# Block 0 of a gated long-convolution and SwiGLU layer: first statistics on one engine, rows normed one by one, and the down products of the first row block in another chunk order

## The chip, the cores and the metric

The kernel runs on one core of a Trainium2 chip. A core has TensorE (PE, matrix products into PSUM), VectorE (DVE), ScalarE (ACT), GpSimd (POOL) and SyncE (SP), which here issues nearly all DMAs. The metric is the device time of one execution in microseconds; the median of several runs is compared. Trace times are microseconds from the start of the span.

## The reference

The input x is 2048 rows of D = 576. Six vectors of length D come from a condition c. The layer is a gated causal convolution followed by a SwiGLU network, each behind a layer norm that is scaled and shifted by those vectors:

```python
mod = (silu(c) @ w_mod)                  # sa, ca, ga, sb, cb, gb
h = layernorm(x) * (1 + ca) + sa
x = x + ga * A(h, k, v, shift_k, ssm_k, ssm_D)
h = layernorm(x) * (1 + cb) + sb
x = x + gb * ((silu(h @ w1) * (h @ w3)) @ w2)     # F = 4608
```

A multiplies h (the gate) with y: kv is k, shifted by four taps, times v; y is kv convolved over the 2048 rows with a filter of its own for each channel, plus kv times ssm_D. The reference does the convolution by FFT.

## The kernel before, in words

**Tiling.** The rows are eight blocks of 256. A block lies in SBUF as 128 partitions by 2 rows (`cc` 0 and 1) by 576. The convolution of a block is done in a transformed domain: `x_spectrum` (X, of kv) and `w_spectrum` (W, of the filter taps) are products with small bases on TensorE, copied out of PSUM by ScalarE (helper `forward`, lines 333 and 336). `v_block` combines W into V on VectorE; `pair` multiplies X and V of two blocks and adds into z; `inverse` (L572) brings z back. The SwiGLU part goes over four row blocks of 512 rows (`r` 0 to 3). `stream` computes h (F in 36 groups of 128, in 9 chunks of four) into `h3`; `down` multiplies h3 with w2 in two halves of 288 columns (`h`), nine chunks each, with w2 in a ring of four chunks.

**Block 0** is `first_block` (L661 to 746). Its instructions on VectorE, ScalarE and TensorE are tied to the order of the program by hand (`in_order`); what comes later is ordered by the framework's scheduler, with costs and due times that `advance` hands out. In program order it does this:

- The bases and taps are made; `warm` (L659) issues products that nobody reads, three, then four after the transposes of the taps (`k_rows`, L394).
- kv is built on VectorE, W of block 0 on TensorE (L333). The first layer norm needs mean and variance of two rows per partition. Row 1 has them from `quick_stats` on VectorE (L495 to L500: two partial statistics, one merge, EPS added, and a power on POOL). Row 0 has them later from `ln_sums` on ScalarE (L469, two passes with accumulators) and `ln_var` and `ln_shift` on POOL.
- X, V and z of block 0 follow, three of the six condition vectors (`mod_piece`, L238, and `arow` L249, `brow` L251), the normed rows `hg` on ScalarE (L723), `inverse`, and the gate on VectorE (L544, L546).
- `k_rows(1)` transposes the taps of block 1. `mod_columns` (L267) makes cb and sb as columns, by 60 matmuls of one column. Then come the four pieces of `w_spectrum(1)`.
- For each row the residual is added (`residual_row`, L579, L581), the second statistics are taken, and `normed` (L504) writes the row into `h2row`, which has 640 columns: the last 64 of the 576 twice. `turn_split` (L611) transposes five tiles of 128 on TensorE; the repeated columns make the fifth tile hold its 64 rows twice, at partitions 0 and 64. `turned_split` scales and shifts out of PSUM into `h2T`, tiles 0 to 2 on ScalarE (L623), 3 and 4 on VectorE (L620). Between them stand `warm` calls of six, two and three.

PSUM is four slots of one shape, given in turn to every product. `stream` for row block 0 then starts (L1014, L1025; h on ScalarE L1032 and L1036, VectorE L1039), with the rest of blocks 1, 2 and 3 on VectorE beside it. Its chunks become complete in the order 4, 5, 6, 0, 7, 1, 8, 2, 3, since six of them are first done for 256 rows alone. `down(0)` (L1134, w2 loaded by L1123) goes through the chunks in the order 0 to 8.

**Queues.** SP issues loads in order; a load waits there until its buffer is free. Transposing DMAs (L303, L819) and spills of X and V (L445, L449) stand in the same queue.

Of the kernel before, what the change touches and what calls it, by code (L numbers as in the profile page):

```python
# [21 lines left out]
H = 288  # L22
NF = F // P
# [4 lines left out]
W2C = 4  # L28
# [7 lines left out]
HEAD_PACE = 1.4  # L36
AHEAD = 2
EPS = 1e-5
TURN = 7
QUICK = False  # L40

# [7 lines left out]
class _Kernel:  # L49
# [205 lines left out]
    def mod_columns(self):  # L255

        nc = self.nc
        w5 = self.wm[:, 0:5 * 6 * D].rearrange("p (a d) -> p a d", a=5)
        ps = self.ps()
        for i, m in enumerate((4, 3)):  # L260
            for j in range(6):
                lo = min(P * j, 512)
                n = P if j < 4 else 64
                out = ps[0:n, i, j:j + 1] if j < 5 else ps[64:P, i, 4:5]
                for ct in range(5):
                    k = P if ct < 4 else 64
                    nc.tensor.matmul(out, w5[0:k, ct, m * D + lo:m * D + lo + n],  # L267
                                     self.crep[0:k, ct, 0:1], start=(ct == 0), stop=(ct == 4))
        nc.scalar.activation(self.cbcol[:], ps[:, 0, 0:5], ACT.Copy, bias=1.0)
        nc.scalar.copy(self.sbcol[:], ps[:, 1, 0:5])  # L270


    def load_kv(self, s, between=None):
# [315 lines left out]
    def normed(self, s, cc, m, r):  # L589

        row, x1 = self.h2row, self.xo[s]
        self.center(row[:, cc, 0:D], x1[:, cc, :], m, r)
        self.center(row[:, cc, D:640], x1[:, cc, 512:D], m, r)

    def normed_act(self, s, cc, r, b):
        row, x1 = self.h2row, self.xo[s]
        with self.behind(self.nc.scalar):
            for lo, hi, at in ((0, D, 0), (512, D, D)):
                self.nc.scalar.activation(row[:, cc, at:at + hi - lo], x1[:, cc, lo:hi], ACT.Identity,  # L599
                                          bias=b[:, cc:cc + 1], scale=r[:, cc:cc + 1])  # L600

    def turn(self, pt, cc):
        for ct in range(5):
            self.nc.tensor.transpose(pt[:, cc, ct * P:(ct + 1) * P],
                                     self.h2row[:, cc, ct * P:(ct + 1) * P], self.ident[:])

    def turn_split(self, cc):

        pt = [self.ps((P, 2, 1024), BF16) for _ in range(2)]
        for ct in range(5):  # L610
            self.nc.tensor.transpose(pt[ct // 3][:, 0, ct % 3 * P:(ct % 3 + 1) * P],  # L611
                                     self.h2row[:, cc, ct * P:(ct + 1) * P], self.ident[:])
        return pt

    def turned_split(self, pt, cc):
# [45 lines left out]
    def first_block(self):  # L661

        nc = self.nc
        since = len(nc.cur_bb.bb.instructions)
        x1 = self.xo[0]
        self.angles(nc.vector, 1)
        self.whole_turns(1)
        self.waves(1)
        self.shift_taps()
        self.whole_turns(0)  # L670

        ps = self.ps()
        nc.tensor.matmul(ps[0:64, 0, 0:5], self.drow[:], self.ident[0:9, 0:9:2], start=True, stop=True)
        nc.tensor.matmul(ps[64:P, 0, 0:4], self.drow[:], self.ident[0:9, 1:9:2], start=True, stop=True)
        nc.scalar.copy(self.dcol[:, 0:4], ps[:, 0, 0:4])
        nc.scalar.copy(self.dcol[0:64, 4:5], ps[0:64, 0, 4:5])
        tap = self.knat[:, :, 0]
        nc.gpsimd.tensor_add(tap, tap, self.dcol[:])
        self.waves(0)
        self.warm(3, self.h2T[0][:, 0, :])  # L680
        sums = [self.small.tile([P, 1], F32, name="l1" + k, tag="sr" + k) for k in "um"]
        self.run_all(self.k_rows(0))
        self.cond_silu()
        self.warm(4, self.h2T[0][:, 0, :])
        rows = self.kv_rows(0)
        for _ in range(4):
            next(rows)

        nc.vector.memset(self.wm[0:1, 3 * D:3 * D + 1], 0.0)
        self.load_mod(3, 2)  # L690
        self.load_k(1)
        self.run_all(self.w_spectrum(0))
        self.cond()
        self.run_all(rows)
        mean, rstd = self.quick_stats(x1[:, 1, :], "l1")
        nmr = self.small.tile([P, 1], F32, name="l1nm", tag="nmr1")
        nc.gpsimd.tensor_mul(nmr[:], mean, rstd)
        nc.gpsimd.tensor_single_scalar(nmr[:], nmr[:], -1.0, op=ALU.mult)
        self.run_all(self.x_spectrum(0))
        self.run_all(self.v_block(0))  # L700
        self.load_w13(0, 0)
        self.load_kv(1)
        self.load_x(1)
        self.load_w13(1, 1)
        self.load_gb()
        self.whole_turns(0, True)
        self.waves(0, True)
        X, V = self.X[0], self.V[0]
        self.accs[0] = z = self.acc.tile([P, 6, D], BF16, name="z0", tag="z0")
        for o in (0, 3):  # L710
            nc.vector.tensor_add(X[:, o, :], X[:, o + 1, :], X[:, o + 2, :])
            nc.vector.tensor_mul(z[:, o:o + 3, :], X[:, o:o + 3, :], V[:, o:o + 3, :])
            nc.vector.tensor_add(z[:, o + 1, :], z[:, o, :], z[:, o + 1, :])
            nc.vector.tensor_sub(z[:, o, :], z[:, o, :], z[:, o + 2, :])
        self.mod_piece(2)
        self.ln_sums(x1, 0, sums[0], sums[1], 0)
        scales = [self.ln_shift(*self.ln_var(*sums, "l1", nc.gpsimd), nc.gpsimd), (rstd, nmr)]
        for m in (1, 0):
            self.mod_piece(m)
        self.hg[0] = hg = self.lnp.tile([P, 2, D], BF16, name="hg", tag="hg", bufs=2)  # L720
        for cc in range(2):
            r, b = scales[cc]
            nc.scalar.activation(hg[:, cc, :], x1[:, cc, :], ACT.Identity, bias=b[:, 0:1], scale=r[:, 0:1])  # L723
        ps = [self.inverse(0, cc) for cc in range(2)]
        self.run_all(self.gate(0))
        self.run_all(self.k_rows(1))
        self.mod_columns()
        self.run_all(self.w_spectrum(1))
        self.residual_row(0, 0, ps[0])
        st = [self.quick_stats(x1[:, 0, :], "l2")]  # L730
        self.residual_row(0, 1, ps[1])
        st.append(self.quick_stats(x1[:, 1, :], "l2"))
        self.normed(0, 0, *st[0])
        busy = self.shk[:, 0, 0:512]
        self.warm(6, busy)
        pt = self.turn_split(0)
        self.warm(2, busy)
        self.normed(0, 1, *st[1])
        self.turned_split(pt, 0)
        pt = self.turn_split(1)  # L740
        self.warm(3, busy)
        self.turned_split(pt, 1)
        self.accs.pop(0)
        self.hg.pop(0)
        self.start = since
        return self.in_order(since, [e.engine for e in (nc.vector, nc.scalar, nc.tensor)])[nc.vector.engine]
# [367 lines left out]
    def down(self, r, rate):  # L1114
        nc = self.nc
        for h in range(2):
# [1 line left out]
            tail = r == NRB - 1 and h == 1  # L1118
            accs = [self.ps() for _ in range(4 if tail else 2)]
            acc = [accs[t][:, 0, 0:H] if tail else accs[t // 2][:, t % 2, 0:H] for t in range(4)]  # L1120
            for f0 in range(0, NF, W2C):
                w = _ap(self.w2m, (h * NF + f0) // W2C % NW2 * W2C * H, [[H, W2C], [1, H]])
                nc.sync.dma_start(w, self.w2[f0 * P:(f0 + W2C) * P, h * H:(h + 1) * H]  # L1123
                                  .rearrange("(a p) d -> p a d", p=P))
                last = f0 + W2C == NF
                if h == 0 and last:
                    self.last_w2 = self.newest()
                order = [(f, t) for f in range(W2C) for t in range(4)]
                if f0 == 0:
                    order = [(f, t) for t0 in (0, 2) for f in range(W2C) for t in (t0, t0 + 1)]  # L1130
                if last:
                    order = [(f, t) for t in range(4) for f in range(W2C)]
                for f, t in order:
                    nc.tensor.matmul(acc[t],  # L1134
                                     self.h3[:, f0 + f, t * P:(t + 1) * P], w[:, f, :],
                                     start=(f0 + f == 0), stop=(f0 + f == NF - 1))
# [12 lines left out]
                self.advance(rate * W2C * 4 * 0.126)  # L1149
# [127 lines left out]
```

## Time and profile before

| what | value |
|---|---|
| median of 5 runs | 510.14 us (509.44 to 510.79) |
| profiled execution | 510.79 us, its span 509.0 us |
| TensorE busy | 491.5 us, 97% of the span |
| VectorE busy | 339.3 us, 67% |
| ScalarE busy | 284.1 us, 56% |
| GpSimd busy | 23.2 us, 5% |
| mean granted clock of TensorE | 0.992 |
| DMA | 107.97 MB, mean 212 GB/s |

The profile is that of one execution. A timeline row gives start, duration, engine, line, operation, what it writes and reads, shapes and count, and in brackets how long the engine stood idle and what ended that. A chain is followed back from the last instruction to what released it. Ends of matmuls are modelled, so matmuls that follow each other overlap in the records: from start to start is the better spacing. The clock column is the share of TensorE's full clock that was granted; in the first 12.5 us it has no record of its own and shows 1.00, although 512-column products there start 0.43 us apart.

### The profile page before, as it was taken

The numbers are of one execution on the slowest core, as the hardware profiler recorded it, in microseconds if no ns is written. First come the engines' busy times: TensorE is split into PE (matmuls) and PEld (weight loads), VectorE is DVE, ScalarE is ACT, GpSimd is POOL, SyncE is SP. The second block draws the span as 40 slices with busy tenths as digits, with TensorE's granted clock in tenths as the row PEclk, the third lists the DMA queues.
The fourth block names the chain that finished last, engine by engine and source line by source line (L and its number), as shares of the span: only waits on it lengthen the run. The fifth ranks groups of instructions, "written<-read, shape, count | busy, mean of one in ns | idle before, by whom it ended". The sixth has DMA issues, their size and how long they took to land.

```text
span 509.0 us, 8873 instructions
## 1 busy us (share of the span) xinstructions
PE 491.5 (97%) x3530; PEld 288.2 (57%) x3530; DVE 339.3 (67%) x448; ACT 284.1 (56%) x565; POOL 23.2 (5%) x43
## 2 busy tenths in 40 slices
PE   6999989999998999999999999999999999999996
PEld 2767865547676444343777543434677544444774
DVE  8789899897998675999157999789771311112012
ACT  5839669758352579578560365975825255555000
POOL 4200000000001000000000000000000000000000
PEclk9979999999999999999999999999999999999999
DMA  8978887658999895448799996735475554460562
GB/s 272 332 199 211 255 315 221 197 176 264 258 366 294 286 315 181 158 109 270 205 272 332 313 319 226 217 104 175 140 188 124 172 176 137 145 187 0 140 171 62
DMA packets 115036, 107.97 MB, mean 212 GB/s; under 512 B 20339, under 2 KB 107572, under 8 KB 114996
## 3 DMA queue, kind: packets, MB, share of 16 engines
q1 hardware_dynamic: 114974, 107.41, 70.3%
q8 instruction: 27, 0.44, 0.4%
q14 instruction: 13, 0.11, 0.1%
q10 hardware_dynamic: 22, 0.01, 0.0%
HBM read 92.46 MB, written 9.44 MB: 200 GB/s over the span
## 4 chain that ended last, share of the span: by engine, by line
PE 63%; DVE 18%; DMA 7%; ACT 6%; issue 3%; SPq 2%; POOL 1%; POOLq 0%; DVEq 0%; ACTq 0%
PE ps L1014 25%; PE ps L1078 14%; PE ps L1134 14%; PE ps L1025 4%; DVE p L438 3%; DMA V<-Vd 2%; DVE z L440 2%; ACT junk L469 2%; DVE h L1039 2%; PE ps L333 2%; DVE z L433 2%; DVE og L1159 1%; PE ps L347 1%; DMA kh<-in_A_k_dram 1%; DMA wst<-in_B_w_dram 1%
## 5 line engine op out<-in xcount | busy, mean ns | idle before, releaser
L1014 PE MATMUL ps<-h2T,wst 128*128 128x512 bf16 (+1 forms) x1056 | 200.8, 341 | 0.9 <-ACT X L349 0.2
L1134 PE MATMUL ps<-wst,h 128*128 128x288 bf16 x1152 | 145.3, 286 | 4.7 <-DMA wst<-in_B_w_dram 3.2
L1014 PEld LDWEIGHTS <-wst 128*128 128x128 bf16 x1056 | 100.2, 98 | 86.8 <-issue 15.3
L1134 PEld LDWEIGHTS <-h 128*128 128x128 bf16 x1152 | 112.4, 98 | 36.2 <-issue 6.2
L1032 ACT ACTIVATE h<-ps 128x512 bf16<-128x512 f32 x108 | 64.8, 600 | 78.9 <-PE ps L1025 50.7
L1078 PE MATMUL ps<-h2T,wst 64*128 64x512 bf16 x648 | 70.3, 376 | 0.0
L1036 ACT CAST u<-ps 128x512 bf16<-128x512 f32 x108 | 63.4, 587 | 0.0
L438 DVE TENSOR_TENSOR p<-X,V 128x3456 bf16<-128x3456 bf16 x28 | 54.8, 1956 | 4.9 <-DMA V<-Vd 3.4
L440 DVE TENSOR_TENSOR z<-z,p 128x3456 bf16<-128x3456 bf16 x28 | 54.7, 1954 | 0.1
L1078 PEld LDWEIGHTS <-wst 64*128 64x128 bf16 x648 | 31.3, 94 | 38.3 <-DVE og L1159 0.2
L1105 DVE TENSOR_TENSOR h<-h,u 128x1024 bf16<-128x1024 bf16 x18 | 12.5, 692 | 58.1 <-ACT u L1102 58.1
L1039 DVE TENSOR_TENSOR h<-h,u 128x1024 bf16<-128x1024 bf16 x54 | 37.0, 687 | 12.9 <-ACT u L1036 12.9
L1099 ACT ACTIVATE h<-ps 128x512 bf16<-128x512 f32 x36 | 21.5, 597 | 39.8 <-PE ps L1078 39.8
L469 ACT ACTIVATE junk<-x 128x576 bf16<-128x576 bf16 x54 | 37.1, 687 | 3.1 <-DVE x L587 2.6
L1159 DVE TENSOR_TENSOR og<-ps,gbrow 128x576 bf16<-128x576 f32 (+1 forms) x18 | 12.3, 689 | 36.2 <-PE ps L1134 35.7
L1025 PE MATMUL ps<-h2T,wst 64*128 64x512 bf16 (+1 forms) x264 | 33.3, 341 | 0.1
L1102 ACT CAST u<-ps 128x512 bf16<-128x512 f32 x36 | 20.9, 581 | 0.0
L1025 PEld LDWEIGHTS <-wst 64*128 64x128 bf16 x264 | 8.5, 94 | 21.5 <-issue 18.1
L834 ACT ACTIVATE h2T<-h2T,sbcol,cbcol 128x256 bf16<-128x256 bf16 x20 | 10.4, 589 | 17.9 <-DMA h2T<-h2row 17.9
L599 ACT ACTIVATE h2row<-x,l2n,l2r 128x576 bf16<-128x576 bf16 (+1 forms) x24 | 13.7, 643 | 10.0 <-DVE l2n L487 10.0
L367 DVE TENSOR_TENSOR kv<-kv,p 128x1152 bf16<-128x1152 bf16 x24 | 18.1, 755 | 0.3
L361 DVE TENSOR_TENSOR p<-kh,shk 128x3456 bf16<-128x3456 bf16 x8 | 15.6, 1953 | 1.1 <-DMA kh<-in_A_k_dram 1.1
(142 smaller groups left out, 368.2 us busy)
## 6 DMA issues: line engine op xcount, KB each, us to landing
wst<-in_B_w_dram SPq DMA_DIRECT2D x80, 512.0 KB, 4.8
wst<-in_B_w_dram SPq DMA_DIRECT2D x72, 288.0 KB, 3.9
wst<-in_B_w_dram SPq DMA_DIRECT2D x80, 64.0 KB, 3.5
kh<-in_A_k_dram SPq DMA_DIRECT2D x7, 720.0 KB, 7.1
X<-Xd SPq DMA_DIRECT2D x5, 864.0 KB, 6.7
V<-Vd SPq DMA_DIRECT2D x5, 864.0 KB, 5.6
Xd<-X SPq DMA_DIRECT2D x4, 864.0 KB, 8.3
Vd<-V SPq DMA_DIRECT2D x4, 864.0 KB, 5.6
```

The lines of the kernel that those rows point to most:

```text
L438: nc.vector.tensor_mul(p[:], X[:], V[:])
L440: nc.vector.tensor_add(z[:], z[:], p[:])
L469: self.nc.scalar.activation(junk[:], src[:, i, :], func, scale=scale, accum_out=out[:, col:col + 1])
L1014: nc.tensor.matmul(gus[k][:, i, a * n:(a + 1) * n], w[:, 5 * i + ct, (fi + a) * P:(fi + a + 1) * P], hT[:, ct, t0:t1], start=(first and ct ...
L1025: nc.tensor.matmul(gus[k][:, i, a * n:(a + 1) * n], w[rows, 4, (fi + a) * P:(fi + a + 1) * P], hT[rows, 4, t0:t1], start=(first and a == 0 ...
L1032: nc.scalar.activation(self.h3[:, f:f + m, t0:t1], gus[k][:, 0, :].rearrange("p (a t) -> p a t", a=m), ACT.Silu)
L1036: nc.scalar.copy(self.u[:, k % 2, :], gus[k][:, 1, :])
L1039: nc.vector.tensor_mul(h3, h3, self.u[:].rearrange("p b (a t) -> p (b a) t", a=m))
L1078: nc.tensor.matmul(gus[k][:, i, :], ws[fc][rows, 5 * i + ct if ct < 4 else 4, cols], hT[rows, ct, :], start=swap == 0 and ct == 4, stop=sw ...
L1099: nc.scalar.activation(h3, gus[k][:, 0, :], ACT.Silu)
L1102: nc.scalar.copy(self.u[:, k % 2, :], gus.pop(k)[:, 1, :])
L1134: nc.tensor.matmul(acc[t], self.h3[:, f0 + f, t * P:(t + 1) * P], w[:, f, :], start=(f0 + f == 0), stop=(f0 + f == NF - 1))
```

## The change

1. Both rows of block 0 have their first statistics from `quick_stats` on VectorE; `ln_sums` on ScalarE and the five small POOL operations behind it go.
2. `mod_columns` multiplies with 64 equal columns instead of one, and reads every 64th.
3. `normed` no longer writes the repeated columns. `turn_tile` transposes the 64 last columns twice, into partitions 0 and 64. `normed_act`, for later blocks, still writes them.
4. In block 0 the order of the residual, the second statistics, the normed rows and `w_spectrum(1)` changes: row 0 is normed before row 1's statistics, two pieces of the spectrum stand ahead of the first turn and two behind it.
5. `warm` calls go from 3, 4, 6, 2, 3 products to 6, 3, 0, 0, 3.
6. `down(0)` goes through the chunks in the order of `FIRST`.

```diff
+FIRST = (4, 5, 6, 0, 7, 1, 8, 2, 3)
...
-                out = ps[0:n, i, j:j + 1] if j < 5 else ps[64:P, i, 4:5]
+                out = ps[0:n, i, 64 * j:64 * j + 64] if j < 5 else ps[64:P, i, 256:320]
...
-                                     self.crep[0:k, ct, 0:1], start=(ct == 0), stop=(ct == 4))
-        nc.scalar.activation(self.cbcol[:], ps[:, 0, 0:5], ACT.Copy, bias=1.0)
-        nc.scalar.copy(self.sbcol[:], ps[:, 1, 0:5])
+                                     self.crep[0:k, ct, 0:64], start=(ct == 0), stop=(ct == 4))
+        nc.scalar.activation(self.cbcol[:], ps[:, 0, 0:320:64], ACT.Copy, bias=1.0)
+        nc.scalar.copy(self.sbcol[:], ps[:, 1, 0:320:64])
...
-        self.center(row[:, cc, D:640], x1[:, cc, 512:D], m, r)
...
+    def turn_tile(self, dst, cc, ct):
+
+        n = P if ct < 4 else 64
+        for at in range(0, P, n):
+            self.nc.tensor.transpose(dst[at:at + n], self.h2row[:, cc, ct * P:ct * P + n], self.ident[:])
...
-        self.warm(3, self.h2T[0][:, 0, :])
-        sums = [self.small.tile([P, 1], F32, name="l1" + k, tag="sr" + k) for k in "um"]
+        self.warm(6, self.h2T[0][:, 0, :])
         self.run_all(self.k_rows(0))
         self.cond_silu()
-        self.warm(4, self.h2T[0][:, 0, :])
+        self.warm(3, self.h2T[0][:, 0, :])
...
-        mean, rstd = self.quick_stats(x1[:, 1, :], "l1")
-        nmr = self.small.tile([P, 1], F32, name="l1nm", tag="nmr1")
-        nc.gpsimd.tensor_mul(nmr[:], mean, rstd)
-        nc.gpsimd.tensor_single_scalar(nmr[:], nmr[:], -1.0, op=ALU.mult)
+        scales = []
+        for cc in range(2):
+            mean, rstd = self.quick_stats(x1[:, cc, :], "l1")
+            nmr = self.small.tile([P, 1], F32, name="l1nm", tag="nmr1")
+            nc.gpsimd.tensor_mul(nmr[:], mean, rstd)
+            nc.gpsimd.tensor_single_scalar(nmr[:], nmr[:], -1.0, op=ALU.mult)
+            scales.append((rstd, nmr))
...
-        self.ln_sums(x1, 0, sums[0], sums[1], 0)
-        scales = [self.ln_shift(*self.ln_var(*sums, "l1", nc.gpsimd), nc.gpsimd), (rstd, nmr)]
...
-        self.run_all(self.w_spectrum(1))
         self.residual_row(0, 0, ps[0])
-        st = [self.quick_stats(x1[:, 0, :], "l2")]
+        st = self.quick_stats(x1[:, 0, :], "l2")
         self.residual_row(0, 1, ps[1])
-        st.append(self.quick_stats(x1[:, 1, :], "l2"))
-        self.normed(0, 0, *st[0])
+        self.normed(0, 0, *st)
         busy = self.shk[:, 0, 0:512]
-        self.warm(6, busy)
+        spectrum = self.w_spectrum(1)
+        for _ in range(2):
+            next(spectrum)
         pt = self.turn_split(0)
-        self.warm(2, busy)
-        self.normed(0, 1, *st[1])
+        self.normed(0, 1, *self.quick_stats(x1[:, 1, :], "l2"))
         self.turned_split(pt, 0)
+        self.run_all(spectrum)
         pt = self.turn_split(1)
...
-            for f0 in range(0, NF, W2C):
+            for n, fc in enumerate(FIRST if r == 0 else range(NF // W2C)):
+                f0 = n * W2C
                 w = _ap(self.w2m, (h * NF + f0) // W2C % NW2 * W2C * H, [[H, W2C], [1, H]])
-                nc.sync.dma_start(w, self.w2[f0 * P:(f0 + W2C) * P, h * H:(h + 1) * H]
+                nc.sync.dma_start(w, self.w2[fc * W2C * P:(fc + 1) * W2C * P, h * H:(h + 1) * H]
...
-                                     self.h3[:, f0 + f, t * P:(t + 1) * P], w[:, f, :],
+                                     self.h3[:, fc * W2C + f, t * P:(t + 1) * P], w[:, f, :],
```

More of the change, by code (lines that the diff above doesn't have):

```diff
@@ L600, in normed_act @@
                                           bias=b[:, cc:cc + 1], scale=r[:, cc:cc + 1])
+    def turn_tile(self, dst, cc, ct):
+        n = P if ct < 4 else 64
+        for at in range(0, P, n):
+            self.nc.tensor.transpose(dst[at:at + n], self.h2row[:, cc, ct * P:ct * P + n], self.ident[:])
     def turn(self, pt, cc):
         for ct in range(5):
-            self.nc.tensor.transpose(pt[:, cc, ct * P:(ct + 1) * P],
-                                     self.h2row[:, cc, ct * P:(ct + 1) * P], self.ident[:])
+            self.turn_tile(pt[:, cc, ct * P:(ct + 1) * P], cc, ct)
     def turn_split(self, cc):
@@ L610, in turn_split @@
         for ct in range(5):
-            self.nc.tensor.transpose(pt[ct // 3][:, 0, ct % 3 * P:(ct % 3 + 1) * P],
-                                     self.h2row[:, cc, ct * P:(ct + 1) * P], self.ident[:])
+            self.turn_tile(pt[ct // 3][:, 0, ct % 3 * P:(ct % 3 + 1) * P], cc, ct)
         return pt
```

## The prediction, made before the changed kernel was built or run

> **What bounds the kernel now.** First I read the chain of work that ended last. It runs through TensorE for nearly the whole of block 0 (to 35 us), so there a saved microsecond of TensorE counts until another engine is later.
>
> ```profile
> 20.78 2.18 PE ps L572 x16
> 22.96 0.56 PE ps L394 x10
> 23.52 3.79 PE ps L267 x60
> 27.30 3.95 PE ps L333 x16
> 31.25 2.21 PE ps L659 x6
> 33.46 0.18 PE ps L611 x3
> ```
>
> Columns: start, us, what. Sixteen matmuls of L333 take 2.07 at 14.52 by the same chain, but 3.95 at 27.30. The windows view says why (columns: window; busy of PE, weight loads, DVE, ACT, POOL; granted clock; DMA share; GB/s):
>
> ```profile
> 19.32:22.73 3.41, 3.41 (x27) 2.29 (x27) 3.31 (x6) 1.18 (x5) 2.56 (x5) 1.00 1.14 330
> 22.73:26.14 3.41, 3.41 (x60) 3.09 (x59) 1.90 (x4) 2.47 (x3) 0.00 (x0) 1.00 1.00 384
> 26.14:29.56 3.42, 3.42 (x25) 2.49 (x26) 3.25 (x8) 1.05 (x4) 0.55 (x1) 0.50 1.11 319
> 29.56:32.97 3.41, 3.41 (x13) 1.66 (x11) 2.39 (x9) 1.73 (x3) 0.66 (x1) 0.50 1.22 222
> 32.97:36.38 3.41, 3.33 (x24) 1.72 (x23) 2.44 (x5) 2.20 (x6) 0.00 (x0) 1.00 0.28 78
> ```
>
> The clock is halved from 26.14 to 32.97, after the stretch filled by mod_columns' one-column matmuls. Third, the timeline of the same place, with what each waited for in brackets:
>
> ```profile
> 22.57 0.87 ACT L723 ACTIVATE hg<-x,l1n,l1r 128x576 bf16<-128x576 bf16 x1 [2.20 <-POOL l1n L487]
> 24.23 0.76 DVE L544 TENSOR_TENSOR hg<-hg,arow 128x1152 bf16<-128x1152 bf16 x1 [1.37 <-ACT hg L723]
> 30.78 0.63 DVE L504 TENSOR_SCALAR h2row<-x,l2mv,l2r 128x576 bf16<-128x576 bf16 x2
> 33.73 2.20 ACT L623 ACTIVATE h2T<-ps,sbcol,cbcol 128x128 bf16<-128x128 bf16 x6 [1.80 <-PE ps L611]
> 33.85 1.28 DVE L620 TENSOR_SCALAR h2T<-ps,cbcol,sbcol 128x128 bf16<-128x128 bf16 x4 [1.57 <-PE ps L611]
> ```
>
> VectorE stands 1.37 us for ScalarE's normed row, and later 1.57 us for the transposes, which stand behind the slow L333 and six L659 fillers. Last, the down stage of row block 0:
>
> ```profile
> 125.39 6.39 PE L1134 MATMUL ps<-wst,h 128*128 128x288 bf16 x50
> 132.91 7.77 PE L1134 MATMUL ps<-wst,h 128*128 128x288 bf16 x62 [1.13 <-DVE h L1039]
> ...
> 156.63 8.00 PE L1134 MATMUL ps<-wst,h 128*128 128x288 bf16 x64 [1.96 <-DMA wst<-in_B_w_dram]
> 164.84 0.38 PE L1014 MATMUL ps<-h2T,wst 128*128 128x512 bf16 x1 [0.21 <-ACT h2T L834]
> ```
>
> After 50 matmuls (three chunks and two) it waits 1.13 for the last gated chunk, which VectorE finishes late; then 1.96 for a weight chunk.
>
> **The parts.**
>
> *Head.* Six fillers from 5.41 instead of three: four 512-column fillers start 0.43 apart (1.71 for 4), so they end near 8.0, before the transposes at 8.58 that wait for POOL: nothing. Three instead of four after k_rows: L333 can start at 10.99, when kT's copy ends (9.87 + 1.12), not 11.33. Its reader is VectorE, which is later by the next part: counted nothing.
>
> *Both first statistics on VectorE.* One set takes 1.17 from start to next instruction (27.16 to 28.33). The second would push L415 from 14.30 to 12.21 + 2 x 1.17 = 14.55. The 0.84 idle before L415 hides most; L422 waited until about 14.81 for a W copy anyway, and now starts at 14.55 + 0.39 = 14.94, 0.08 late. So all of z is 0.08 late, and brow (22.10) goes to 22.18. On ScalarE two passes of 0.70 and two reads of about 0.2 go; on POOL five operations (0.94, 0.41, 0.43, 0.59, 0.19) go, and three (0.56, 0.19, 0.39), early and unhurried, come. hg now follows ga: 18.24 + 0.66 + two of 0.86 = about 20.6, before brow ends. L544 then starts at 22.18 + 0.67 = 22.86 instead of 24.23: **-1.37 on VectorE**. What is late next is brow, VectorE's own work.
>
> *Residual and second norm on VectorE.* The same spacing as before puts L579 for row 0 at 24.51, its statistics at 25.79, L579 for row 1 at 26.96. POOL's power ends 27.7; the first normed row starts at 28.24 (29.61 - 1.37) and costs 0.43 without the repeated columns (0.30 less, twice). The second set now stands behind it: 28.58 to 29.83; power to 30.58, a wait of about 0.75 before the second normed row at 30.61. Behind that wait stand the two turned pieces, then kv_rows(1). Normed ends 31.04; turned(0)'s two at 30.97 and 31.23.
>
> *TensorE.* mod_columns ends near 27.3, or 27.0 if its last part is not at half clock. A one-column matmul takes 63 ns (3.79 / 60) and a 128-column one 56 (0.56 / 10), so columns hardly set the price: 0, with -0.35 and +1.6 (27 ns more on each of 60) as ends. The Trainium skill, "TensorE: Matmul & The Clock Gate", section "Back-to-back issue gap", puts 1 to 64 columns at one price; by it the sum is 0 as well. Two pieces of L333 (8 matmuls, half of 2.07) fit from 27.3 to 28.3; the second needs PSUM that L579 frees at 27.7. Turn 0 waits for VectorE until 28.7. The other two pieces fill 29.1 to 30.1. Turn 1 waits for VectorE: 31.1, its last tiles 31.6 (bank freed by turned(0)). Twelve transposes for ten: two of 56 ns, hidden in that wait. Eight fillers (6 and 2) go; the last three are hidden by ScalarE.
>
> *ScalarE.* W copies end 29.1; turned(0) 29.1 to 30.3; W copies to 31.4; turned(1) 31.4 to 32.6 (three, 0.34 apart). The stream flows from there, where it did at 35.95: 3.3 earlier. VectorE starts kv_rows(1) at about 32.5, not 35.05: 2.5 earlier. Up to 66 us both count, x_spectrum joining them near 44; I take **-2.6**, ends -2.4 and -3.3. In stream 0's second half the normed rows of block 1 lose 0.29 twice, before a wait for kh at 64.85: nothing.
>
> *Down in chunk order.* The 1.13 wait goes, as the late chunks 2 and 3 come eighth and ninth, 14 us on (7 x 1.96). Late next is w2: its loads wait behind SP's transposing DMAs (issued 129.96 to 133.10), and the seventh chunk's load leaves at 133.20 for about 5.4 to landing, as before. After that the DMA wait of 1.96 at 156.63 can simply grow, with DMA share near 1. What comes through is bounded by 0 and -1.29 (with the semaphore's time); nearest is the turn at 164.84, whose chain had VectorE idle 0.77 for inverse L572: I take **-0.3**.
>
> Sum against the profiled execution (span 509.0, time 510.79): -2.6 - 0.3 = -2.9, 507.9. That execution lies 0.65 over the median 510.14, so the median of the runs becomes about 507.2.
>
> **The clock, and a rule against the change.** 288 columns stream in 0.1225 us, so 64 take 27 ns: about 0.4 of mod_columns' time, against 0.006 with one column. The window 152.44 to 155.86, with 18 matmuls of 288 columns (2.2 of 3.4 us), kept clock 1.00, so I take the clock to hold; 0.4 itself is not shown. At 23 us ten transposes run 56 ns apart at clock 1.00. The same page, "Part 4: PE-mode transpose", says that transposes don't count as TensorE activity the same way. By it the stretch after 29.5, where real fillers give way to transposes and waits, could let the clock fall: the sum would be the first rival's, not the forecast; no row separates the two.
>
> **Rivals.**
> 1. *The clock halves anyway.* For it: 0.4 is below what any window shows kept. Then the first two pieces end at 29.2, turn 0 at 29.8, the other two pieces at 31.8, the stream starts at 33.6, and may run at half to 36.4 (cost half of 2.8, 1.4). Gain 2.3 to 0.9, with the 0.3 or without: median 507.5 to 509.2, say 508.6.
> 2. *A transfer takes the place.* In the first 32 us the DMA share is about 1.0, and VectorE already waits 0.31 for kh at 64.85. If that load (issued 57.91, 6.92 to landing) does not move, the wait grows by all of the gain: about 510. Against: SP's waits from 36 to 66 us are 10.2 of L965 for TensorE, so loads move with TensorE.
> 3. *Slower: the order after block 0.* From 36 us the framework's schedule sets it, and it may come out otherwise. The place is VectorE between 143.9 and 157, on the chain to the turn at 164.84: two products of 1.95 already stand in it. Each further one ahead of L487 costs 1.95 there, one for one as TensorE waits for that turn. One leaves 0.95 of the gain; from two on it is slower: +1.0, median 511.1. Against: nothing in the change names these instructions.
>
> **Numbers.** Forecast 0.60 (505.6 to 507.7); rival 1: 0.17; rival 2: 0.13, which is also the case that block 0's end was covered; rival 3: 0.10. A measurement tells 0.2% (1.0 us) from nothing. Faster 0.60 + 0.17 = 0.77, within 0.13, slower 0.10. The low end is -3.3 - 1.29 from 510.14, 505.6; the high end reaches over rival 1 and most of rival 2, 510.0.
>
> **What would show it.** Clock 1.00 from 26 to 36 us; L544 at about 22.9 with no wait for ScalarE; first stream matmul near 32.6, L361 near 32.5; no wait for h L1039 in the first down stage, but longer ones for w2. Wrong if the clock row shows 0.50 there, if kh's wait at 64.85 grows, or if the turn's landing near 164 stays.

## The result, and the profile after

| | before | after |
|---|---|---|
| median of the runs | 509.91 us (507.16 to 512.72, 80 runs) | 508.21 us (505.85 to 511.14, 43 runs) |
| profiled execution, its span | 510.79 us, 509.0 us | 506.55 us, 504.7 us |
| mean granted clock of that execution | 0.992 | 0.999 |

The ratio of after to before is 0.9964 [0.9956, 0.9972]: the change makes the kernel 0.36% faster, about 1.8 us (the two medians lie 1.7 apart). The forecast for the median was 2.9 us less. The two profiled executions lie 4.24 us apart, more than twice the distance of the medians, because before's was taken 0.9 above its median and after's 1.7 below. So this pair of traces must not be read as the result, and below several profiles of each kernel stand side by side.

Line numbers move a little: L333, L394, L267, L572 and L659 of before are L334, L395, L268, L573 and L663 in after, L544 is L545, L504 is L505, L620 is L624, L361 is L362, L1039 is L1043, the transposes of block 0's rows (L611) are L606, and the matmuls of `stream` and `down` (L1014, L1134) are L1018 and L1139.

The chain of waits of after at the end of block 0 (start, us, what) answers to the one of before:

```profile
23.00 0.56 PE ps L395 x10
23.56 4.28 PE ps L268 x60
27.83 0.61 PE ps L334 x4
28.46 0.67 ACT W L337 x2
```

The chain no longer stays on TensorE. Sixteen matmuls of the spectrum at half clock and six fillers stood behind `mod_columns` before. Now the chain leaves TensorE for ScalarE at 28.4. But the 60 matmuls of `mod_columns` take 4.28 us in this view, where they took 3.79 with their last part at half clock. The windows of the same stretch (window; busy of PE, weight loads, DVE, ACT, POOL; granted clock; DMA share; GB/s):

```profile
22.66:26.07 3.41, 3.41 (x52) 2.74 (x50) 3.20 (x6) 1.12 (x1) 0.00 (x0) 1.00 1.01 378
26.07:29.49 3.42, 3.35 (x39) 2.39 (x37) 3.26 (x10) 1.25 (x4) 0.56 (x1) 1.00 1.11 324
29.49:32.90 3.41, 3.12 (x24) 1.60 (x23) 2.27 (x7) 3.33 (x9) 0.55 (x1) 1.00 1.31 218
```

The clock column reads 1.00 where before had 0.50 for two windows. In this execution it is 1.00 until 503.9, 0.8 us before the end. VectorE in the same place:

```profile
22.81 0.75 DVE L545 TENSOR_TENSOR hg<-hg,arow 128x1152 bf16<-128x1152 bf16 x1
28.07 0.42 DVE L505 TENSOR_SCALAR h2row<-x,l2mv,l2r 128x576 bf16<-128x576 bf16 x1
30.32 0.43 DVE L505 TENSOR_SCALAR h2row<-x,l2mv,l2r 128x576 bf16<-128x576 bf16 x1 [0.66 <-POOL l2r L501]
31.72 0.59 DVE L624 TENSOR_SCALAR h2T<-ps,cbcol,sbcol 128x128 bf16<-128x128 bf16 x2 [0.47 <-PE ps L606]
32.23 1.95 DVE L362 TENSOR_TENSOR p<-kh,shk 128x3456 bf16<-128x3456 bf16 x1
```

L545 starts at 22.81 and waits for nothing. The wait for the second POOL power (0.66) and the one for the last transposes (0.47) are new places, but short. L362 starts at 32.23, where it did at 35.05. Last, the down stage of row block 0 on TensorE:

```profile
122.05 13.88 PE L1139 MATMUL ps<-wst,h 128*128 128x288 bf16 x112
...
149.22 2.12 PE L1139 MATMUL ps<-wst,h 128*128 128x288 bf16 x16 [1.37 <-DMA wst<-in_B_w_dram]
152.33 8.00 PE L1139 MATMUL ps<-wst,h 128*128 128x288 bf16 x64 [0.99 <-DMA wst<-in_B_w_dram]
160.17 0.38 PE L1018 MATMUL ps<-h2T,wst 128*128 128x512 bf16 x1
160.80 2.12 PE L1139 MATMUL ps<-wst,h 128*128 128x288 bf16 x16 [0.25 <-DMA wst<-in_B_w_dram]
```

The first 112 matmuls, seven chunks, run through: the wait of 1.13 for h is gone. In its place the second half waits three times for w2, 2.61 together, where before had one wait of 1.96.

### The profile page after: what moved, and what is told of

Its sections match the earlier page's. It is cut to its first block, busy times and chain, and to the rows that moved or that the text cites. A ratio compares the mean times of both kernels' runs of the same rounds, so it can differ in the third digit from the quotient of the medians.

```text
span 504.7 us, 8868 instructions
## 1 busy us (share of the span) xinstructions
PE 487.8 (97%) x3528; PEld 286.0 (57%) x3528; DVE 339.1 (67%) x448; ACT 282.3 (56%) x561; POOL 22.3 (4%) x41
## 4 chain that ended last, share of the span: by engine, by line
PE 62%; DVE 20%; DMA 6%; ACT 5%; issue 3%; SPq 2%; POOL 1%; POOLq 0%; DVEq 0%; ACTq 0%
PE ps L1018 26%; PE ps L1139 15%; PE ps L1082 14%; PE ps L1029 4%; DVE p L439 3%; DMA V<-Vd 2%; DVE z L441 2%; DMA kh<-in_A_k_dram 2%; DMA wst<-in_B_w_dram 2%; ACT junk L470 2%; DVE z L434 2%; DVE og L1164 2%; DVE h L1043 1%; PE ps L348 1%; SPq L823 1%
## 5 line engine op out<-in xcount | busy, mean ns | idle before, releaser
L1018 PE MATMUL ps<-h2T,wst 128*128 128x512 bf16 (+1 forms) x1056 | 200.6, 341 | 0.4 <-ACT X L350 0.2
L1139 PE MATMUL ps<-wst,h 128*128 128x288 bf16 x1152 | 145.4, 286 | 4.0 <-DMA wst<-in_B_w_dram 3.5
L1018 PEld LDWEIGHTS <-wst 128*128 128x128 bf16 x1056 | 100.2, 98 | 86.3 <-issue 14.5
L1139 PEld LDWEIGHTS <-h 128*128 128x128 bf16 x1152 | 112.5, 98 | 35.2 <-issue 6.4
L1043 DVE TENSOR_TENSOR h<-h,u 128x1024 bf16<-128x1024 bf16 x54 | 37.0, 687 | 12.7 <-ACT u L1040 12.7
L470 ACT ACTIVATE junk<-x 128x576 bf16<-128x576 bf16 x52 | 35.7, 687 | 3.1 <-DVE x L588 2.6
L362 DVE TENSOR_TENSOR p<-kh,shk 128x3456 bf16<-128x3456 bf16 x8 | 15.6, 1954 | 1.0 <-DMA kh<-in_A_k_dram 1.0
## 6 DMA issues: line engine op xcount, KB each, us to landing
wst<-in_B_w_dram SPq DMA_DIRECT2D x80, 512.0 KB, 4.8
```

The source lines that it names most:

```text
L470: self.nc.scalar.activation(junk[:], src[:, i, :], func, scale=scale, accum_out=out[:, col:col + 1])
L1018: nc.tensor.matmul(gus[k][:, i, a * n:(a + 1) * n], w[:, 5 * i + ct, (fi + a) * P:(fi + a + 1) * P], hT[:, ct, t0:t1], start=(first and ct ...
L1043: nc.vector.tensor_mul(h3, h3, self.u[:].rearrange("p b (a t) -> p (b a) t", a=m))
L1139: nc.tensor.matmul(acc[t], self.h3[:, fc * W2C + f, t * P:(t + 1) * P], w[:, f, :], start=(f0 + f == 0), stop=(f0 + f == NF - 1))
```

## The experiments

**How they are read.** The first product of each `kv_rows` (L361 in before) stands at a fixed place in every kernel, so the time from one to the next splits the span into stretches. Below, "0 to 1" is the time from that product of block 0 to that of block 1, and so on. The stretch 2 to 3 (38.48 or 38.49) and the stretch 6 to 7 (33.74 to 33.76) are the same in all of them to 0.02 us, and are left out; "to the end" is from the product of block 0 to the end of the span. The clock column lists the windows of 3.41 us of half clock found in the trace; a piece of one in the last 2.5 us of the span, which most traces have, is left out. All in us, from one profiled execution each.

| kernel | 0 to 1 | 1 to 2 | 3 to 4 | 4 to 5 | 5 to 6 | 7 to end | to the end | half-clock windows |
|---|---|---|---|---|---|---|---|---|
| before | 28.56 | 29.80 | 55.02 | 52.03 | 99.23 | 165.64 | 502.51 | 2 in block 0 |
| before_again | 28.50 | 30.13 | 54.52 | 52.34 | 99.46 | 166.39 | 503.57 | 2 in block 0 |
| first_only | 28.31 | 30.20 | 54.15 | 52.53 | 100.03 | 165.75 | 503.21 | 2 in block 0 |
| stats_only | 27.35 | 29.47 | 54.45 | 52.17 | 99.06 | 165.79 | 500.52 | 1 in block 0 |
| order_only | 26.78 | 30.22 | 54.44 | 52.07 | 99.34 | 165.44 | 500.53 | 2 in block 0 |
| block0_only | 26.76 | 29.84 | 54.72 | 52.55 | 99.81 | 165.55 | 501.47 | 1 in block 0 |
| one_col | 25.87 | 29.41 | 54.51 | 53.73 | 100.53 | 165.32 | 501.61 | 1 in block 0, 1 in down |
| after | 25.77 | 29.29 | 53.61 | 52.45 | 99.34 | 165.57 | 498.26 | none |
| after_second | 26.88 | 29.35 | 54.56 | 52.58 | 98.94 | 165.48 | 500.04 | 1 in block 0 |
| after_third | 25.79 | 29.24 | 53.61 | 52.28 | 98.56 | 165.62 | 497.34 | none |
| split_cols | 27.67 | 29.45 | 54.46 | 52.05 | 98.76 | 165.22 | 499.84 | 1 in block 0 |
| split_w13 | 27.82 | 29.40 | 53.61 | 50.37 | 98.90 | 165.53 | 497.87 | 1 in block 0 |
| after_w13 | 26.73 | 29.66 | 53.92 | 50.46 | 98.69 | 165.61 | 497.31 | 1 in block 0 |
| late_w13 | 26.09 | 30.16 | 53.79 | 60.56 | 99.39 | 165.27 | 507.49 | 1 in block 0, 2 from 175 |

**before_again**: the kernel before, run as if it were a change.

> The kernel before, unchanged, as a control: its two profiles so far would tell how much one execution differs from the next. The two profiled executions of before and of the changed kernel lie 4.24 us apart (510.79 and 506.55), the medians only 1.7 (509.91 and 508.21). Theory A (the free-running clock makes the difference): here the granted clock differs from run to run, some runs without the halved stretch after mod_columns (mean clock about 0.999) and about 1 to 1.5 us faster than those at 0.992 or 0.993. Theory B (the transfers scatter): the clock is 0.992 to 0.994 in nearly all runs, and the times still spread over 4 us. Ratio 1.000 by both.

Measured: 0.9997 [0.9973, 1.0021]. An interval of 12 runs reaches 0.24% to either side, so a single term of 0.3 us can't be seen by times here; the stretches of the table carry more. Neither theory came out whole: none of the 12 runs has a mean clock of 0.998 or more, so none kept the full clock, as the first had expected of some; but the six at 0.993 or less take 512.0 on the average and the six others, at 0.995 to 0.997, 510.0.

**first_only**: before, with the chunk order alone.

```diff
-            for f0 in range(0, NF, W2C):
+            for n, fc in enumerate(FIRST if r == 0 else range(NF // W2C)):
+                f0 = n * W2C
```

> The kernel before with the down products of row block 0 in chunk order alone. The prediction's term: -0.3 us (bounds 0 and -1.29), ratio 0.9994 (0.9975 to 1.000). Rival, read from the changed kernel's profile, where the turn moved 4.67 us and the start of the down stage 3.34: -1.3, ratio 0.9975. By both the wait for h L1039 in the first down stage is gone; by the first the later waits for w2 chunks grow from 1.96 to about 3 us, by the second they stay near 2.

Measured: 0.9981 [0.9962, 1.0], which leaves anything from 0 to a gain of 2 us. The trace decides more. TensorE's waits in the down stage of row block 0:

```profile
137.61 2.12 PE L1136 MATMUL ps<-wst,h 128*128 128x288 bf16 x16 [0.38 <-DMA wst<-in_B_w_dram]
...
152.08 2.12 PE L1136 MATMUL ps<-wst,h 128*128 128x288 bf16 x16 [0.44 <-DMA wst<-in_B_w_dram]
156.10 8.00 PE L1136 MATMUL ps<-wst,h 128*128 128x288 bf16 x64 [1.90 <-DMA wst<-in_B_w_dram]
```

No wait for h is left, but the weights are waited for 2.72 in all, against 1.13 for h and 1.96 for w2 in before (0.73 for h and 2.28 for w2 in before_again). That is the growth which the prediction's term expected. The stretch from 3 to 5 is 106.68, where before had 107.05 and before_again 106.86.

**block0_only**: after, with the down products in the old order.

```diff
-            for n, fc in enumerate(FIRST if r == 0 else range(NF // W2C)):
+            for n, fc in enumerate(range(NF // W2C)):
```

> The changed kernel with the down products in the old chunk order. The prediction's term: -2.6 us (-2.4 to -3.3), ratio 0.995. Rival (the median of the changed kernel moved 1.7 us, so block 0 is worth less later): the same 2.8 to 3.3 us at the start of the stream in row block 0, but only -0.5 to -1.5 at the end, ratio 0.997 to 0.999, with the rest lost where the down stage waits for w2 or for h L1039.

Measured: 0.9970 [0.9951, 0.9989], in the recorded rival's range rather than at 0.995. Block 0 alone gives as much as the whole change, within these intervals. Its down stage has the waits of before again:

```profile
130.34 7.77 PE L1139 MATMUL ps<-wst,h 128*128 128x288 bf16 x62 [0.94 <-DVE h L1043]
...
153.94 8.00 PE L1139 MATMUL ps<-wst,h 128*128 128x288 bf16 x64 [1.96 <-DMA wst<-in_B_w_dram]
```

The stretch from 3 to 5 is 107.27 here. Five profiles without the new chunk order (before, before_again, stats_only, order_only, block0_only) have 107.05, 106.86, 106.62, 106.51 and 107.27, mean 106.86; the three of after have 106.06, 107.14 and 105.89, mean 106.36, and first_only 106.68; one_col has 108.24, with a half-clock window in that stage. split_cols below, which has the new order too, has 106.51. The six with the new order have a mean of 106.75, or 106.46 without one_col. The order removes one wait and makes others, and what is left, 0.1 to 0.4 us of these means, is smaller than the scatter of this stage.

**one_col**: after, with `mod_columns` at one column again.

```diff
-                out = ps[0:n, i, 64 * j:64 * j + 64] if j < 5 else ps[64:P, i, 256:320]
+                out = ps[0:n, i, 64 * j:64 * j + 1] if j < 5 else ps[64:P, i, 256:257]
...
-                                     self.crep[0:k, ct, 0:64], start=(ct == 0), stop=(ct == 4))
+                                     self.crep[0:k, ct, 0:1], start=(ct == 0), stop=(ct == 4))
```

> The changed kernel with mod_columns at one column again (read at the same places). If the 64 columns hold the clock (the prediction): the granted clock halves for 3.4 to 6.8 us from about 26, mean clock 0.993 to 0.996, the stream starts at about 33.6 instead of 32.4 to 33.1, and the kernel is 1 to 2 us slower than the changed one, ratio 0.998 to 1.000. Rival (VectorE bounds the end of block 0 whatever the clock is): the clock halves, but the stream starts within 0.5 us of the changed kernel's, ratio 0.996.

Measured: 0.9959 [0.9938, 0.9980], not slower than after. `mod_columns` and the pieces of the spectrum in the chain of waits, and the window in which the clock halved:

```profile
23.08 3.56 PE ps L268 x60
26.64 1.41 PE ps L334 x8
28.93 1.95 PE ps L334 x8
```

```profile
23.85:27.26 3.41, 3.41 (x52) 3.00 (x52) 3.13 (x9) 0.78 (x3) 0.56 (x1) 1.00 1.06 368
27.26:30.68 3.42, 3.40 (x18) 1.85 (x17) 2.69 (x9) 3.01 (x6) 0.55 (x1) 0.50 1.10 321
```

The clock does halve, for one window. Yet 0 to 1 takes 25.87, 0.10 more than in after with the clock full. That is what the recorded rival had put, but its reason does not show: the chain of one_col stays on TensorE from 20.65 until the stream, so VectorE does not bound it. What the same view shows is one price against another: 60 matmuls of one column take 3.56, 60 of 64 columns 4.28 in after and block0_only, both at full clock. So the 64 columns cost about 0.7 us of TensorE ahead of everything that follows. Counted from the first product of block 0, one_col starts the pieces of the spectrum 0.7 earlier than after, and with the clock halved there its first stream matmul comes 0.2 later (26.00 and 25.80). The columns do change the clock: over the timed runs, 9 of 12 of one_col and all 12 of order_only have a mean granted clock of 0.993 or less, 1 of 44 of after. But in the time of the kernel nothing of it can be measured, with an interval of 0.2% to either side.

**stats_only**: before, with both first statistics on VectorE and nothing else.

```diff
-        mean, rstd = self.quick_stats(x1[:, 1, :], "l1")
+        scales = []
+        for cc in range(2):
+            mean, rstd = self.quick_stats(x1[:, cc, :], "l1")
...
-        self.ln_sums(x1, 0, sums[0], sums[1], 0)
-        scales = [self.ln_shift(*self.ln_var(*sums, "l1", nc.gpsimd), nc.gpsimd), (rstd, nmr)]
```

> The kernel before with both first statistics on VectorE, and nothing else. The prediction's part: L544 1.37 us earlier on VectorE. But in the old order the transposes of block 0's rows wait for TensorE (four pieces of L333 at half clock and six fillers), so I expect the stream's start and kv_rows(1) within 0.3 us of before, counted from the first kv_rows: ratio 0.999 to 1.000. Rival: the 1.37 us come through, ratio 0.9973.

Measured: 0.9991 [0.9969, 1.0012], and 27.35 for 0 to 1 in the profile, 1.2 less than before. By the timed runs nothing is shown; the profile's gain I had not expected. VectorE has L544 at 22.72 without a wait, so the saving is there, and TensorE is what had to hold it back:

```profile
27.16 3.41 PE ps L333 x16
30.57 1.29 PE ps L659 x6
```

The same rows of the chain read 3.95 and 2.21 in before. In this execution the clock was halved for one window (26.46 to 29.87) instead of two, and the two rows are 0.54 + 0.92 = 1.46 shorter, which is more than the 1.2. So the gain of that profile is one of the clock, not of the statistics, as far as one profile can say.

**order_only**: after without the statistics, the 64 columns and the chunk order; what stays is the order of block 0, the rows without repeated columns, the split turn and the fillers.

```diff
-        scales = []
-        for cc in range(2):
-            mean, rstd = self.quick_stats(x1[:, cc, :], "l1")
...
+        mean, rstd = self.quick_stats(x1[:, 1, :], "l1")
...
+        self.ln_sums(x1, 0, sums[0], sums[1], 0)
+        scales = [self.ln_shift(*self.ln_var(*sums, "l1", nc.gpsimd), nc.gpsimd), (rstd, nmr)]
...
-            for n, fc in enumerate(FIRST if r == 0 else range(NF // W2C)):
+            for n, fc in enumerate(range(NF // W2C)):
```

> The changed order of residual, second statistics, spectrum and turns, the rows without repeated columns and the moved fillers, without the statistics on VectorE, without the 64 columns and without the chunk order. If the two parts of block 0 are needed together: about half of the 2.7 us, -1.2 to -1.5, since VectorE then starts 1.37 us later; ratio 0.997 to 0.998. Rival (the order alone does it): -2.5, ratio 0.995.

Measured: 0.9987 [0.9965, 1.0008], so the timed runs alone show nothing; in the profile 0 to 1 is 26.78, 1.75 less than in the two profiles of before, with two windows of half clock (26.56 to 33.39) as there. That lies between the two numbers on record. VectorE's rows:

```profile
23.05 0.76 DVE L545 TENSOR_TENSOR hg<-hg,arow 128x1152 bf16<-128x1152 bf16 x1 [1.38 <-ACT hg L727]
32.40 0.60 DVE L624 TENSOR_SCALAR h2T<-ps,cbcol,sbcol 128x128 bf16<-128x128 bf16 x2 [0.91 <-PE ps L606]
```

The wait for ScalarE's normed row is back (1.38), yet most of this stretch's gain is there. So far as one profile separates them, the fillers and pieces of the spectrum that stood ahead of the turns were what the end of block 0 waited for in before. Here the chain of waits runs instead through POOL's power of the first statistics, ScalarE's `hg` and VectorE's L545 to the first normed row at 28.40, so now the statistics are late. They come on top: one_col, which is this kernel with both statistics on VectorE and the new chunk order, has 25.87, 0.91 less. Some of that may again be the clock, halved for one window there.

**after_second and after_third**: the changed kernel again, for a single profiled execution and for 12 timed runs.

> The changed kernel, a second profiled execution. If the scatter of the runs is that of the transfers in the down stages, the part from the first kv_rows to the second is 25.8 (clock held) or about 26.8 us (clock halved in mod_columns), the part from the third to the fourth exactly 38.48, and the parts from the fourth to the sixth differ from the first profile's 53.61 and 52.45 by up to 1 us. If it is the clock, those parts repeat within 0.2 us, and only the clock's stretches differ.

> The changed kernel once more, on the chip of these runs, timed. 0.9964 as before (0.995 to 0.998). First to second kv_rows either 25.8 with the clock held through 36 us, or 26.7 to 26.9 with a halved stretch, and nothing between.

Measured: 508.03 us for the single execution; 0.9968 [0.9949, 0.9987] for the third, its profiled execution 505.42 us. The second is the telling one. Its windows:

```profile
23.57:26.99 3.42, 3.42 (x50) 2.58 (x48) 3.18 (x8) 0.91 (x1) 0.20 (x1) 1.00 1.04 376
26.99:30.40 3.41, 3.41 (x21) 2.16 (x21) 2.64 (x8) 1.47 (x5) 0.91 (x2) 0.50 1.11 318
```

It is the same program, with 64 columns, and the clock halves all the same, after a window that began 0.47 us behind the first matmul of `mod_columns`; in after it began 0.73 ahead of it. 0 to 1 is 26.88, 1.1 more. Half clock for one window takes 0.0034 off the mean clock of a run, the piece at the end of the span at most 0.0024 in these traces. By the mean clock, which is listed for each run, 24 of 44 runs of after have 0.998 or more (mean 507.7 us) and 19 have 0.994 to 0.997 (mean 508.65 us), like after_second's 0.995. By these means a window of half clock costs 0.94 us, give or take 0.6 by the spread of the runs, and comes in 20 of 44 runs: 0.43 us on the average. Of 94 runs of before, 45 have 0.993 or less, like its profiled 0.992 with two windows.

**split_cols**: one column, with the two halves of `mod_columns` apart, the first ahead of `inverse`, so that no window should hold one-column matmuls alone.

```diff
+        self.mod_columns(0)
...
-        self.mod_columns()
+        self.mod_columns(1)
```

> The changed kernel with mod_columns at one column and cut in two: the 30 products of one vector ahead of inverse, where TensorE stands about 1.2 us for z, the other 30 where they were. If a window of the clock falls when it holds too little streaming, whatever the columns, no window now holds more than 2 us of one-column work: the clock holds at 1.00, or its fall no longer matters since TensorE is some 1.5 us ahead; first to second kv_rows 25.8 in this profile (26.8 or 26.9 in the profiles of the changed kernel and of the old chunk order with a fall), ratio 0.995 to 0.996. Rival (the fall comes anyway and still costs): 26.5 to 27.

Measured: 0.9974 [0.9953, 0.9995]; 0 to 1 is 27.67, worse than after by 1.9. It fails in two ways, which three rows show:

```profile
21.71 1.89 PE L270 MATMUL ps<-crep,h 64*128 64x1 bf16 x26 [0.31 <-DMA h<-in_w_mod_dram]
23.54 3.41 PE L577 MATMUL ps<-z,Fb 128*128 128x288 bf16 x16
```

```profile
25.67 0.76 DVE L584 TENSOR_TENSOR hg<-ps,hg 128x576 bf16<-128x576 f32 x1 [1.80 <-PE ps L577]
```

The first half comes before its weights have landed. The clock then halves from 22.77 to 26.19, just under `inverse`, whose 16 matmuls take 3.41, and VectorE waits 1.80 for them. Here it was better for the halved window to fall on the spectrum's pieces.

**late_w13, split_w13, after_w13**: a part that the change does not touch. The waits of the second half of `down(0)` stand behind one load of row block 1's stream weights (the second chunk, 1.15 MB, issued between 139 and 144 in before and between 135 and 141 in after, among the loads of w2). late_w13 is one_col with that load tied behind the newest instruction of SP; the two others are split_cols and after with it tied behind the last w2 load of `down(0)`:

```diff
+                elif r == 1 and fc == 1:
+                    with self.tc.issue_after(self.end_w2):
+                        self.load_w13(fc, buf)
...
+                if last:
+                    self.end_w2 = self.newest()
```

> The changed kernel with one column in mod_columns, and the load of the second weight chunk of row block 1 (1.15 MB, issued amid the w2 loads of the first down stage) put behind the loads of that stage. If that load is what makes the w2 chunks of the second half late (TensorE waits 1.4 to 2.1 us there in each profile), the waits fall under 0.5 us and the kernel is 1 to 1.5 us faster than the one-column kernel: ratio 0.993 to 0.994. Rival (the spills of X and the transposes do it, or TensorE waits for the turn in any case): waits and time as before, ratio 0.996. If the load is then late itself, TensorE waits for it at about 177 us, ratio above 0.996.

> The same, with the second weight chunk of row block 1 loaded right behind the last w2 load of the first down stage, ahead of the loads that made it 8.3 us late in the other try. If the w2 waits of the second half are made by that load: waits there under 1 us, fourth to fifth kv_rows 53.8 or less, no wait of 8 us near 170, ratio 0.993 to 0.994. Rival (the bytes only move): the chunk, or X<-Xd, which now stands later in the queue, is awaited instead, ratio 0.996 or above.

> The changed kernel with nothing but the second weight chunk of row block 1 loaded right behind the last w2 load of the first down stage. If the parts add up: the changed kernel's 0.9966 less the 0.0039 that this step made on the cut mod_columns (0.9935 against 0.9974), so 0.992 to 0.993; fourth to fifth kv_rows 53.6 (as in the two faster profiles of the changed kernel), fifth to sixth 50.4 instead of 52.3 to 52.6. Rival (the step only makes the slow profiles of the down stage like the fast ones): 53.6 and 52.3, ratio 0.995.

Measured: late_w13 1.0155 [1.0126, 1.0184], split_w13 0.9935 [0.9907, 0.9963], after_w13 0.9936 [0.9912, 0.9959] with a median of 505.75 us. In late_w13 the load leaves too late, and TensorE stands for it:

```profile
159.22 2.12 PE L1139 MATMUL ps<-wst,h 128*128 128x288 bf16 x16 [0.68 <-DMA wst<-in_B_w_dram]
...
179.12 3.25 PE L1018 MATMUL ps<-h2T,wst 128*128 128x512 bf16 x8 [8.29 <-DMA wst<-in_B_w_dram]
```

The waits for w2 did shrink to 0.68, so the cause was rightly named, but the chunk, issued from 172.6 on, costs a wait of 8.29. In after_w13 the load is issued from 158.3 to 160.7, which is early enough:

```profile
145.30 14.07 PE L1144 MATMUL ps<-wst,h 128*128 128x288 bf16 x112
159.93 2.12 PE L1144 MATMUL ps<-wst,h 128*128 128x288 bf16 x16 [0.56 <-DMA wst<-in_B_w_dram]
```

Seven chunks of the second half run through, one wait of 0.56 is left, and 4 to 5 takes 50.46 where it took 52.03 to 52.58 in the kernels without the edit, one_col apart. after_w13 beats both kernels; against after, the distance of the two ratios is 0.28%, and their intervals overlap by 0.03%, though split_w13 against split_cols (0.9935 and 0.9974, with one stretch of the table changed in the same way) points to the same.

## Why the prediction was right or wrong, point by point

**The number.** The median 508.21 lies within the range as a whole, but outside the 505.6 to 507.7 that had 0.60 and inside the band of the first rival, 507.5 to 509.2, which had 0.17. Measured against before, the gain is 1.8 of the 2.9 forecast. The points below say how far the mechanism goes the same way.

**Block 0, -2.6: right where the clock holds.** From 0 to 1 the two profiles of after at full clock have 25.77 and 25.79, before 28.56 and 28.50: 2.75 less. Step by step, L545 was put at 22.86 and came at 22.81. The first normed row was put at 28.24 and came at 28.07, the second at 30.61 and came at 30.32, with a wait of 0.66 for POOL's power where 0.75 was forecast. The first stream matmul was put at 32.6 and came at 32.26, L362 at 32.5 and came at 32.23. What the first two parts were worth beside each other was not worked out in the prediction; in one profile of order_only the order and the fillers alone make 1.75 of it, which its timed runs neither show nor exclude.

**The 64 columns at a price of 0, with the clock taken to hold: the step that was mis-sized.** The prediction drew the price from 63 ns for a one-column and 56 ns for a 128-column matmul, but the row of 63 ran with its last part at half clock. At full clock the same view has 71 ns with 64 columns (4.28 / 60) against 59 with one (3.56 / 60), about 0.7 us in all, inside the end of +1.6 that was given. The Trainium skill, "TensorE: Matmul & The Clock Gate", section "Back-to-back issue gap", has one price for 1 to 64 columns; with these 60 matmuls, each with its own weight load, the trace does not agree, and the measurement decides. The second half of the step, "I take the clock to hold", was true in 24 of 44 runs, as their mean clocks tell. The others pay about 0.94, which is the first rival in part: it had the clock low until 31.8 and perhaps to 36.4, and the traces show a single window of 3.41, to 30.4 in after_second. Price and windows together are why one_col, with neither the cost nor the clock, is no slower than after.

**Down in chunk order, -0.3: not seen.** The wait for h went as the step says, in first_only and in the three profiles of after. That the wait of 1.96 "can simply grow" is what happened: w2 is waited for 2.61, 3.00 and 2.39 in the three profiles of after and 2.72 in first_only, against 1.96 and 2.28 in the two of before. The stretch from 3 to 5 has a mean of 106.75 with the order (106.46 without one_col) and 106.86 without, while single profiles lie 1 us apart. The forecast 0.3 is inside that; whether it is 0 or 0.3 stays open, and the interval of first_only does not settle it.

**The sum.** Put by terms: -2.75 for block 0 at full clock, +0.43 for the clock on the average, 0 for down, makes -2.3 against a before with two windows of half clock, as its profile has. But 49 of 94 runs of before have one such window or none, by their mean clock. Those with two or more have a mean of 510.64 us, all others 509.8, so the mean of before is itself some 0.4 below what the prediction's working, drawn from one profile, took for it. That leaves -1.9, beside the measured -1.8. The last two steps are averages and not a measurement of their own, and the sum leaves out the stretch from 1 to 2. There the prediction counted the shorter normed rows of block 1 at nothing; yet that stretch is 29.24 to 29.35 in the three profiles of after and 29.80 and 30.13 in before, 0.5 to 0.9 less. With it the sum would be -2.4 to -2.8, so the agreement to 0.1 is not to be leaned on, and why the timed runs show less than the profiles' stretches stays open.

**Rival 2, a transfer takes the place: fell.** VectorE's wait for kh, 0.31 at 64.85 in before, is 0.16 at 61.52 in after. The load moved with TensorE, from 57.91 to 54.87. This wait scatters: it is 0.64 in before_again, 0.71 in block0_only, 0.23 and 0.12 in the other two profiles of after. **Rival 3, another order after block 0: fell.** The instructions behind block 0 stand in the same order on SP in both kernels, and on VectorE, ScalarE and POOL differ only by the repeated columns that are no longer written. **Signs to look for.** The clock 1.00 from 26 to 36 showed in two of three profiles, L545 without a wait for ScalarE and no wait for h in all. The first stream matmul came at 32.26 and 31.80 where the clock held, and at 33.06 in after_second.

**What stays open.** What the clock asks of a window is not settled (the last section). Nor is the scatter of the down stage: 3 to 4 took 53.61 in after, after_third and split_w13, but 54.56 in after_second, from the same program. All of it is behind loads, and nothing tried here separates it.

## What to carry to other kernels

Where the clock falls in a stretch, its cost is a few windows of half clock times the chance that they come, so look at several profiled executions and at the mean clock of each timed run before a term is priced. An edit that fills the windows has its own price in the same stretch: here 64 columns cost TensorE about 0.7 us, against some 1 us for a halved window, and the kernel without them is no slower. Taking idle products and late work off the chain made 1.75 of the 2.75 us of block 0 in a profile; the times could not tell the parts of block 0 from each other. Where a wait for a ring of weights remains after its first cause is gone, look for what else was issued on the same queue among the loads; moving one load of 1.15 MB behind them took the ratio from 0.9964 to 0.9936, with intervals that barely overlap, and the stretch 4 to 5 from 52.5 to 50.5.

## What the runs showed of the hardware that I had not expected

The granted clock moves in steps of 3.41 us that are the same grid all through an execution but lie elsewhere against the work in the next: the fall comes at 26.14 in before, 27.26 in one_col, 26.99 in after_second, and in after not before 503.9. The value is 0.50 or 1.00. The Trainium skill, "TensorE: Matmul & The Clock Gate", section "What's actually happening", gives a free-running window of 3413 ns and no values between; these traces agree.

How full a window must be is only bracketed. My estimate of a window's fill is its streamed columns at 0.1225 us for 288, over 3.41. Windows at 0.07 to 0.23, filled by one-column matmuls without a gap (PE busy 3.41 of 3.41), were followed by half clock. So was 0.36 in after_second and after_w13, 0.39 in block0_only and 0.42 in split_cols. But 0.39 and 0.42 also held, in the down stages of block0_only and split_cols, and 0.45 held in after_third and 0.50 in after. So the 0.4 of the prediction stands right at the edge, and neither this estimate nor the busy share of the profile tells the two sides apart.

By the chain a one-column matmul of `mod_columns` stood 59 ns from the next, one of 64 columns 71 (74 in after_second, where the last part ran at half clock). The timeline gives the same difference, 0.71 us for 60, from the first start to the next line's first: 22.92 to 26.58 in one_col, 23.39 to 27.76 in after. A profile's own time lay up to 2.8 us from its kernel's median: 510.79 for 509.91, 506.55 and 505.42 for 508.21.
